# A sliding-window attention and ReGLU kernel: two more Strassen pairs from the third tiles of the last four halves, early scores for two halves, packed masks

## The chip, the cores and the metric

The kernel runs on one core of a Trainium2 chip. The metric is device time in microseconds of one launch; the time before is the median of three runs. The core has a matmul engine (TensorE, PE in the profile; PEld is its weight load), a vector engine (VectorE, DVE), a scalar engine (ScalarE, ACT), GpSimd (POOL) and SyncE (SP, which here issues DMAs). Each works through its own queue in program order; semaphores tie them together. Matmuls write to PSUM banks, of which there are eight; DVE and ACT read them and write to SBUF.

## The reference

```python
def _attn_ref(q, k, v, n_global, n_local):        # q, k, v: 4 x 8 heads x 768 x 64
    scores = scale * np.matmul(q, k.transpose(0, 1, 3, 2))
    rel = pos[:, None] - pos[None, :]
    is_global = pos[None, :] < int(n_global)       # 8
    is_local = (rel >= 0) & (rel < int(n_local))   # 96
    keep = is_global | is_local
    dist = np.where(is_global & ~is_local, float(n_local), np.abs(rel))
    scores = scores + (-slopes[:, None, None] * dist[None, :, :])[None, :, :, :]
    a = softmax(np.where(keep, scores, -1e9))
    return np.matmul(a, v)

def _moe_ref(x, w_gate, w_val, w_out):             # x: 3072 x 512, d_ff 1536
    gate = np.maximum(x @ w_gate, 0.0)
    val = x @ w_val
    return gate * val @ w_out
```

The attention's output, heads side by side, is `x`. Inputs and output are float32; the kernel multiplies in bf16.

## The kernel before

**Halves and stages.** The 3072 rows are cut into eight halves of 384 rows, numbered 0 to 7 here (the sixth and the eighth half are 5 and 7); two halves make one batch. A half is three tiles of 128 rows. After a hand-ordered opening (halves 0 and 1), the loop `for c in range(2, NHALF)` runs one stage for each half c: the FFN of half c, with the attention of half c+1 and the key and query preparation of half c+2 woven in between. What follows calls these stages 2 to 7.

**Weaving.** `weave` takes the FFN's pieces, each with a weight, and lists of other pieces, each with a place between 0 and 1. After every FFN piece it issues all pieces whose place times the stage's total weight has been reached. `spread(items, a, b)` puts n items at even distances from a to b. This sets the program order, and so the order in every engine's queue. A piece of weight 0.0 costs no place.

**FFN of a half** (`ffn_pieces`). `f1` holds, for each of 12 hidden tiles `fc`, `gate(fc)` (four matmuls of 384 columns, L518, then a relu on ACT, L525) and `val(fc)` (four matmuls, then DVE's `ht = val * relu`, L531). Its first pieces are `begin` (the first three matmuls of gate 0 and val 0, weight 1.0) and the two last matmuls of gate 0 and val 0 (0.15 each). `f2` is the output product. From half 1 on, tiles 0 and 1 are a Strassen pair: seven block products `p4 p3 p1 p2 p5 p6 p7` of six 256-column matmuls each (L583), whose operands are sums of `ht` (`sum_cb`, `sum_ad`, `sum_de` on DVE, L567 to L577) and sums of the output weights (`bs`, made once). ACT copies p4, p3 and p1 into the output rows (L599 to L607), DVE adds p2, p5, p6 and p7 (L611 to L629), p6 onto p3's bank and p7 onto p1's. Some of the sums are issued behind `val` of given hidden tiles (`behind`), the rest inside `f2`. The third tile takes the plain way, `outp`: four parts of three 512-column matmuls (L538), an ACT copy (L543) and a store on SP.

**Attention of a half** (`attention_pieces`): 26 pieces. For each of four head pairs p: `piece_qk` with g = 0, 1, 2 (`pair_scores` issues the score matmuls of both groups into four banks, L397; g = 0 issues the exps of group 0, g = 1 those of group 1 and the masks of group 0, g = 2 the masks of group 1), `piece_av` for both heads (L427, then a log on ACT, L436, and after the second head an exp of the negated log, L441), and `piece_norm` (two DVE multiplications into `xT`, L446). The masks are DVE multiplications of the exponentials with `m_all`, one for each key block, L359: two for each group in an even half, three and two in an odd one. `early_pieces` casts k and q on POOL (L363), transposes them by DMA on SP (L368) and orders the keys on POOL (L259 to L265).

**Buffers.** From the loop on, PSUM is three `ff` banks (gates, values, outp, p4, p3, p1) and five `x` banks (scores, attention sums, p2, p5), each given out in rotation: the fourth `ff` tile waits until the first has been read. `es` (exponentials) has three buffers a group, `ht` two, `osb` (output rows) three.

Of the kernel before, what the change touches and what calls it, by code (L numbers as in the profile page):

```python
# [8 lines left out]
FP32 = mybir.dt.float32  # L9
BF16 = mybir.dt.bfloat16  # L10
# [5 lines left out]
def kernel(  # L16
# [80 lines left out]
    dd = const.tile([128, 2, NN, WQ], BF16)  # L97
# [75 lines left out]
    kq0 = firstp.tile([128, 2, H, NN * D], FP32, name="kq0")  # L173
    kq1 = setupp.tile([128, 2, H, NN * D], BF16, name="kq1")
# [173 lines left out]

    def masks(s, p, g, steps=steps_of):
        for j in steps[s % 2][g]:  # L350
            _, a, w, m = by[s % 2, j]
            es, c = es_of[s, p, j]
            for_all = es[:, :, c : c + NN * w]
            mk = m_all[:, 2 * p : 2 * p + 2, 0 if j == 0 else 1, :, m : m + w]
            if w == WQ:
                mk = mk.rearrange("k e n p -> k e (n p)")
            else:
                for_all = for_all.rearrange("k e (n p) -> k e n p", n=NN)
            nc.vector.tensor_mul(for_all, for_all, mk)  # L359
# [148 lines left out]

    def ffn_pieces(c):
# [43 lines left out]

        N2, D2 = N_FC // 2, DM // 2
        tiles_ = [slice(n * 128, (n + 1) * 128) for n in range(2)]

        def sums_of(name, *shape):
            if name not in st:
                st[name] = late["sums"].tile([128, *shape], BF16, name=name)
            return st[name]  # L560

        cb = lambda: sums_of("cb", N2, 2, 128)
        ad = lambda: sums_of("ad", N2, 128)
        de = lambda: sums_of("de", N_FC, 128)

        def sum_cb(i0, i1):
            nc.vector.tensor_tensor(cb()[:, i0:i1].rearrange("f i n t -> f i (n t)"), ht[:, i0:i1, 0:256],  # L567
                                    ht[:, N2 + i0 : N2 + i1, 0:256], op=ALU.add)

        def sum_ad(i0, i1):  # L570
            nc.vector.tensor_tensor(ad()[:, i0:i1], ht[:, i0:i1, tiles_[0]],
                                    ht[:, N2 + i0 : N2 + i1, tiles_[1]], op=ALU.add)

        def sum_de(i0, i1):
            x, y = (1, 0) if i0 < N2 else (0, 1)
            nc.vector.tensor_tensor(de()[:, i0:i1], ht[:, i0:i1, tiles_[x]], ht[:, i0:i1, tiles_[y]],
                                    op=ALU.subtract)  # L577

        def block(key, pool, left, right, start, stop):
            if start:  # L580
                st[key] = psum[pool].tile([128, 512], FP32, name=f"{pool}_ps")
            for i in range(N2):
                nc.tensor.matmul(st[key][:, 0:D2], lhsT=left(i), rhs=right(i),  # L583
                                 start=start and i == 0, stop=stop and i == N2 - 1,
                                 skip_group_check=not start)
            return st[key][:, 0:D2]

        c0, c1 = slice(0, D2), slice(D2, DM)
        bs = lambda name: lambda i: late["bs"][name][:, i]
        V2 = nc.vector.tensor_tensor  # L590

        def store(n, cols, eng=nc.sync):
            eng.dma_start(out=out_v[c, n][:, cols], in_=st["r", n][:, cols])

        def p4():
            for n in range(2):
                st["r", n] = late["osb"].tile([128, DM], FP32, name="osb")
            ps = block("d", "ff", lambda i: ht[:, N2 + i, tiles_[1]], bs("b21-b11"), True, True)
            nc.scalar.copy(st["r", 0][:, c0], ps)  # L599

        def p3():
            ps = block("c", "ff", lambda i: ht[:, i, tiles_[0]], bs("b12-b22"), True, True)
            nc.scalar.copy(st["r", 0][:, c1], ps)

        def p1():
            ps = block("a", "ff", lambda i: ad()[:, i], bs("b11+b22"), True, True)
            nc.scalar.copy(st["r", 1][:, c1], ps)  # L607

        def p2():
            ps = block("b", "x", lambda i: cb()[:, i, 1], lambda i: wo_sb[:, i, c0], True, True)  # L610
            V2(st["r", 1][:, c0], ps, st["r", 0][:, c0], op=ALU.add)  # L611
            V2(st["r", 1][:, c1], st["r", 1][:, c1], ps, op=ALU.subtract)

        def p5():
            ps = block("e", "x", lambda i: cb()[:, i, 0], lambda i: wo_sb[:, N2 + i, c1], True, True)
            V2(st["r", 0][:, c1], ps, st["r", 0][:, c1], op=ALU.add)
            V2(st["r", 0][:, c0], st["r", 0][:, c0], ps, op=ALU.subtract)
            if c == NHALF - 1:
                store(1, c0)
                store(0, c1)  # L620

        def p6():
            ps = block("c", "ff", lambda i: de()[:, i], bs("b11+b12"), False, True)
            V2(st["r", 1][:, c1], ps, st["r", 1][:, c1], op=ALU.add)
            store(1, slice(0, DM) if c < NHALF - 1 else c1, nc.sync if c < NHALF - 1 else nc.scalar)

        def p7():
# [251 lines left out]
```

## Time and profile before

| | |
|---|---|
| time, median of 3 runs | 241.64 us (241.13 to 242.92) |
| the profiled execution | 241.74 us, of which the span from first to last instruction is 239.9 us |
| TensorE clock granted | 0.998 |
| PE busy | 233.5 us (97%), 1937 matmuls |
| DVE, ACT, POOL busy | 173.3, 153.4, 85.9 us |
| stage 2 | 78.6 to 104.8 us |
| stage 3 | 104.8 to 131.7 us |
| stage 4 | 131.7 to 159.4 us |
| stage 5 | 159.4 to 186.4 us |
| stage 6 | 186.4 to 213.9 us |
| stage 7 and the end | 213.9 to 239.9 us |

In a row of the profile stand the source line, the engine, the operation, the tile written and the tiles read, the shapes, the count; then the busy time and the mean duration in ns of one; then the engine's idle time before these instructions and what ended it. In a timeline, the first number is the start in us and the second how long the run of equal instructions took. A duration holds the pipeline's latency, so instructions of one engine overlap by it; the distance between starts is what a queue pays. Matmul ends are modelled. A stage's borders here are the starts of its first gate matmul and of the next stage's.

### The profile page before, as it was taken

To read this page: it belongs to the slowest core of one execution; us is meant where nothing else is said; L and a number is where in the kernel's file an instruction comes from. 1 tells how busy PE (TensorE), PEld (TensorE's weight loads), DVE (VectorE), ACT (ScalarE), POOL (GpSimd) and SP (SyncE) were. 2 spreads that over 40 slices of the span, in tenths; PEclk is the share of its full clock that TensorE was granted. 3 is DMA by queue.
4 is the path that set the end of the run, shared out by engine and by line. 5 is a ranking of instruction groups with operands and counts; after the bars stand their busy time and mean duration, and the time that the engine had idled before them with its cause. 6 is when DMAs were issued, how large, how long until landed. Compare 5 with 4: busy or idle time off the path is not lost.

```text
span 239.9 us, 5355 instructions
## 1 busy us (share of the span) xinstructions
PE 233.5 (97%) x1937; PEld 146.6 (61%) x1945; DVE 173.3 (72%) x456; ACT 153.4 (64%) x347; POOL 85.9 (36%) x202
## 2 busy tenths in 40 slices
PE   7899999999999999999999999999999999999994
PEld 3655555665458566666668566676658566676663
DVE  7775955869677788777787687866887677764643
ACT  5897883337775777748774777638774677733330
POOL 6767893208414860903274060902350000000000
PEclk9999999999999999999999999999999999999999
DMA  6999999993976997098519939398431200030003
GB/s 200 181 198 177 257 234 219 185 162 61 270 178 134 301 150 131 8 185 257 108 25 122 285 93 133 19 166 262 67 68 44 90 0 0 3 129 3 4 27 104
DMA packets 69603, 31.42 MB, mean 131 GB/s; under 512 B 47160, under 2 KB 66616, under 8 KB 69576
## 3 DMA queue, kind: packets, MB, share of 16 engines
q0 software_dynamic: 31744, 8.71, 35.3%
q1 hardware_dynamic: 36616, 21.45, 35.1%
q10 hardware_dynamic: 1216, 0.92, 1.2%
q8 instruction: 15, 0.25, 0.4%
q14 instruction: 12, 0.10, 0.1%
HBM read 28.41 MB, written 6.29 MB: 145 GB/s over the span
## 4 chain that ended last, share of the span: by engine, by line
PE 91%; ACT 3%; DVE 2%; issue 1%; ACTq 0%
PE ff_ps L518 53%; PE ff_ps L538 9%; PE ff_ps L583 8%; PE x_ps L427 6%; PE x_ps L397 4%; PE x_ps L583 3%; PE t_ps L459 2%; PE s_ps L341 2%; PE t_ps L272 1%; PE t_ps L682 1%; ACT lnd L436 1%; PE t_ps L310 1%; DVE xT L446 1%; PE s_ps L321 1%; ACT rcp L441 0%
## 5 line engine op out<-in xcount | busy, mean ns | idle before, releaser
L518 PE MATMUL ff_ps<-xT,wg 128*128 128x384 bf16 x384 | 80.7, 326 | 0.5 <-ACT grelu L525 0.4
L518 PE MATMUL ff_ps<-xT,wv 128*128 128x384 bf16 x384 | 80.2, 326 | 0.0
L531 DVE TENSOR_TENSOR ht<-ff_ps,grelu 128x384 bf16<-128x384 f32 x96 | 53.1, 554 | 28.5 <-PE ff_ps L518 13.8
L525 ACT ACTIVATE grelu<-ff_ps 128x384 bf16<-128x384 f32 x96 | 47.1, 492 | 39.4 <-PE ff_ps L518 20.9
L518 PEld LDWEIGHTS <-wg 128*128 128x128 bf16 x384 | 35.9, 98 | 23.9 <-issue 0.9
L518 PEld LDWEIGHTS <-wv 128*128 128x128 bf16 x384 | 36.1, 97 | 23.4 <-issue 1.2
L406 ACT ACTIVATE es<-x_ps 128x360 bf16<-128x360 f32 (+2 forms) x96 | 36.8, 444 | 16.9 <-PE x_ps L397 16.8
L359 DVE TENSOR_TENSOR es<-es,m_all 128x432 bf16<-128x432 bf16 (+4 forms) x108 | 31.2, 334 | 8.2 <-ACT es L406 7.8
L446 DVE TENSOR_TENSOR xT<-x_ps,rcp 64x384 bf16<-64x384 f32 x48 | 26.6, 554 | 9.4 <-ACT rcp L441 8.8
L436 ACT ACTIVATE lnd<-x_ps 64x384 f32<-64x384 f32 x48 | 23.3, 485 | 12.5 <-PE x_ps L427 11.8
L538 PE MATMUL ff_ps<-wo_sb,ht 128*128 128x512 bf16 x112 | 29.6, 379 | 0.4
L363 POOL CAST kqc<-ks 128x384 bf16<-128x384 f32 x24 | 11.6, 532 | 32.3 <-DMA ks<-in_k_dram 32.3
L137 POOL DMA_DIRECT2D vbuf<-in_v_dram x25 | 21.6, 880 | 2.6 <-DMA wv<-in_moe_w_val_dram 2.1
L427 PE MATMUL x_ps<-es,vbuf 128*128 128x216 bf16 (+4 forms) x216 | 21.8, 225 | 0.0
L427 PEld LDWEIGHTS <-vbuf 128*128 128x128 bf16 x216 | 15.8, 97 | 7.7
L538 PEld LDWEIGHTS <-ht 128*128 128x128 bf16 x120 | 10.8, 97 | 9.8 <-issue 0.2
L263 POOL COPY kT<-kqT 128x240 bf16<-128x240 bf16 x16 | 6.9, 430 | 23.0 <-DMA kqT<-kqc 20.5
L363 POOL CAST kqc<-qs 128x384 bf16<-128x384 f32 x24 | 11.6, 522 | 8.1 <-DMA qs<-in_q_dram 8.1
L259 POOL COPY kT<-kqT 128x360 bf16<-128x360 bf16 x10 | 6.0, 604 | 19.9 <-DMA kqT<-kqc 19.9
L441 ACT ACTIVATE rcp<-lnd 128x384 f32<-128x384 f32 x24 | 12.6, 524 | 0.7
L347 ACT ACTIVATE ef<-s_ps 128x720 bf16<-128x720 f32 (+2 forms) x16 | 10.9, 710 | 2.1 <-PE s_ps L341 1.8
L397 PE MATMUL x_ps<-kqT,kT 64*128 64x216 bf16 (+4 forms) x216 | 11.8, 224 | 0.2
(115 smaller groups left out, 252.8 us busy)
## 6 DMA issues: line engine op xcount, KB each, us to landing
out_dram<-osb SPq DMA_DIRECT2D x22, 256.0 KB, 2.7
ks<-in_k_dram SPq DMA_DIRECT2D x6, 768.0 KB, 5.5
qs<-in_q_dram SPq DMA_DIRECT2D x6, 768.0 KB, 12.1
vbuf<-in_v_dram POOLq DMA_DIRECT2D x21, 120.0 KB, 7.9
wg<-in_moe_w_gate_dram POOLq DMA_DIRECT2D x3, 512.0 KB, 7.9
wv<-in_moe_w_val_dram POOLq DMA_DIRECT2D x3, 512.0 KB, 9.8
wo_sb<-in_moe_w_out_dram POOLq DMA_DIRECT2D x1, 1536.0 KB, 19.6
kq<-in_q_dram ACTq DMA_DIRECT2D x2, 192.0 KB, 4.7
```

Source lines behind the costliest of these rows:

```text
L137: nc.gpsimd.dma_start(out=v_dst(b, NG + r0, NG + r0 + n, j), in_=v[b, :, KT * j + r0 : KT * j + r0 + n, :].rearrange("h p d -> p h d"))
L359: nc.vector.tensor_mul(for_all, for_all, mk)
L363: nc.gpsimd.tensor_copy(kqc[:, :, i].rearrange("t n (h d) -> t h n d", d=D)[:, 2 * p : 2 * p + 2], of[s][:, 2 * p : 2 * p + 2, :].rearrang ...
L406: nc.scalar.activation(es[:, e, 0:c], banks[e][:, 0:c], AF.Exp, bias=0.0, scale=scale)
L427: nc.tensor.matmul(av3[:, :, a : a + w], lhsT=vb[:, j, z0 : z0 + 128], rhs=es[:, e, c : c + NN * w].rearrange("k (n p) -> k n p", n=NN), s ...
L436: nc.scalar.activation(ln[o0 : o0 + 64], av[d0 : d0 + 64, 0:QH], AF.Ln, bias=0.0, scale=1.0)
L446: nc.vector.tensor_tensor(xT_of[s][r, p, :], av_of[s, p, e][r, 0:QH], av_of[s, p, "r"][r], op=ALU.mult)
L518: nc.tensor.matmul(st[key][:, 0:QH], lhsT=w_of(w, dc, fc), rhs=xT_of[c][:, dc, :], start=(dc == 0), stop=(dc == N_DC - 1))
L525: nc.scalar.activation(gr, psg[:, 0:QH], AF.Relu, bias=0.0, scale=1.0)
L531: nc.vector.tensor_tensor(ht[:, fc, :], psv[:, 0:QH], st["gr", fc], op=ALU.mult)
L538: nc.tensor.matmul(ps2, lhsT=ht[:, fc, n * 128 : (n + 1) * 128], rhs=wo_sb[:, fc, :], start=(fc == 0), stop=(fc == N_FC - 1))
L583: nc.tensor.matmul(st[key][:, 0:D2], lhsT=left(i), rhs=right(i), start=start and i == 0, stop=stop and i == N2 - 1, skip_group_check=not s ...
```

## The change

- For halves 4 and 6 (`PAIRED`), the third tile is no longer multiplied in its own stage. Stage 4 keeps `third_of[4]`, and stage 5 multiplies the third tiles of halves 5 and 4 as one more Strassen pair; likewise 7 and 6. The sums of that pair have their own buffers (`sums3`); three of the five are issued behind `val` 1, 6 and 7, two at the head of `f2`, whose products go before those of tiles 0 and 1. Stages 4 and 6 have no `outp` left, begin their output products with p3 instead of p4, and put p4 into an `x` bank.
- In stages 3 and 5 the first three attention pieces of halves 5 and 7 (head pair 0: scores, exps and masks) are issued at places 0.82 to 0.93, one stage sooner. The remaining 23 pieces lie at 0 to 0.74 of stages 4 and 6, where 26 lay at 0 to 0.8.
- From half 3 on, the masks of a first score group are one multiplication with a packed copy of the masks. POOL makes the two packed copies once, in five pieces, at places 0.7 to 0.9 of the combined stage of halves 0 and 1 (57 to 78 us).
- `osb` gets a fourth buffer, and the tile `dd` moves to a pool that is closed before the loop.

```diff
+    def pack_mask(half, i):
+        todo = [by[half, j] for j in steps_later[half][0]]
+        if half not in packed_of:
+            packed_of[half] = late["packed"].tile([128, H, sum(NN * t[2] for t in todo)], BF16, name=f"packed{half}")
+        c = sum(NN * t[2] for t in todo[:i])
+        j, _, w, m = todo[i]
+        nc.gpsimd.tensor_copy(
+            packed_of[half][:, :, c : c + NN * w].rearrange("k h (n t) -> k h n t", n=NN),
+            m_all[:, :, 0 if j == 0 else 1, :, m : m + w])
+
     def masks(s, p, g, steps=steps_of):
+        if s > 2 and g == 0:
+            mk = packed_of[s % 2][:, 2 * p : 2 * p + 2]
+            es = es_of[s, p, steps[s % 2][0][0]][0][:, :, 0 : mk.shape[2]]
+            nc.vector.tensor_mul(es, es, mk)
+            return
         for j in steps[s % 2][g]:
...
+    def strassen(pair, sums, bare=False):
+        N2, D2 = N_FC // 2, DM // 2
+        st = {}
+        last = pair[0][0] == NHALF - 1 and pair[0][2] == 0
+        def h(i, f0, f1):
+            _, ht, n = pair[i]
+            return ht[:, f0:f1, n * 128 : (n + 1) * 128]
...
+        def sum_cb_of(i):
+            V2(cb()[:, :, i], h(i, 0, N2), h(i, N2, N_FC), op=ALU.add)
...
+        def p4():
+            ps = block("d", "x" if bare else "ff", lambda i: h(1, N2 + i, N2 + i + 1)[:, 0], bs("b21-b11"), True, True)
+            nc.scalar.copy(rows(0)[:, c0], ps)
...
+        return sum_cb, sum_cb_of, sum_ad, sum_de, [(0.65, f) for f in (((p3, p4) if bare else (p4, p3)) + (p1, p2, p5, p6, p7))]
+
+    PAIRED = (4, 6)
+    third_of = {}
...
+        plain = range(NN) if c < 1 else () if c - c % 2 in PAIRED else (NN - 1,)
+        sum_cb, _, sum_ad, sum_de, products = strassen([(c, ht, 0), (c, ht, 1)], "sums", c in PAIRED)
         behind = {2: [lambda: sum_de(0, 3)], 5: [lambda: sum_de(3, 6)], 8: [lambda: sum_cb(0, 3)],
                   9: [lambda: sum_ad(0, 3)], 10: [lambda: sum_de(6, 9)]}
+        rest = (lambda: sum_ad(3, 6), lambda: sum_cb(3, 6), lambda: sum_de(9, 12))
+        if c in PAIRED:
+            third_of[c] = ht
+        elif c - 1 in PAIRED:
+            _, cb3, ad3, de3, products3 = strassen([(c, ht, NN - 1), (c - 1, third_of[c - 1], NN - 1)], "sums3")
+            behind[1] = [lambda: cb3(1)]
+            behind[6] = [lambda: ad3(0, N_FC // 2)]
+            behind[7] = [lambda: de3(0, N_FC // 2)]
+            rest = (lambda: cb3(0), lambda: de3(N_FC // 2, N_FC)) + rest
...
         if c >= 1:
-            f2 += [(0.65, f) for f in (p4, p3, p1, p2, p5, p6, p7)]
-            for at, f in ((5, lambda: sum_de(9, 12)), (3, lambda: sum_cb(3, 6)), (2, lambda: sum_ad(3, 6))):
+            f2 += (products3 if c - 1 in PAIRED else []) + products
+            places = (2, 3, 5) if plain else (0, 1, 2) if c in PAIRED else (0, 1, 2, 3, 4)
+            for at, f in list(zip(places, rest))[::-1]:
                 f2.insert(at, (0.0, f))
...
-    late["osb"] = ctx.enter_context(tc.tile_pool(name="osb", bufs=3, reuse_waits="tile"))
+    late["osb"] = ctx.enter_context(tc.tile_pool(name="osb", bufs=4, reuse_waits="tile"))
...
+          spread([(0.0, lambda half=half, i=i: pack_mask(half, i)) for half, i in ((1, 0), (1, 1), (1, 2), (0, 0), (0, 1))],
+                 0.7, 0.9))
+
+    ahead = {}
     for c in range(2, NHALF):
         placed = []
-        if c + 1 < NHALF:
-            placed.append(spread(attention_pieces(c + 1), *((0.07, 0.82) if c == 2 else (0.0, 0.8))))
         if c + 2 < NHALF:
             load_qk(c + 2, 0, H)
             load_v_half(c + 2)
             placed.append(spread(early_pieces(c + 2), 0.25, 0.75))
+        if c + 1 < NHALF:
+            pieces = ahead.pop(c + 1, None) or attention_pieces(c + 1)
+            placed.append(spread(pieces, *(0.07, 0.82) if c == 2 else (0.0, 0.74) if c in PAIRED else (0.0, 0.8)))
+        if c + 1 in PAIRED:
+            ahead[c + 2] = attention_pieces(c + 2)
+            placed.append(spread([ahead[c + 2].pop(0) for _ in range(3)], 0.82, 0.93))
         f1, f2 = ffn_pieces(c)
         weave(f1 + f2, *placed)
```

Block products, copies, combinations and stores of `strassen` are otherwise those of before, for the two tiles named in `pair`.

## The prediction

> **What bounds the kernel now.** I read the page first: busy shares and the chain that ended last.
>
> ```profile
> PE 233.5 (97%) x1937; PEld 146.6 (61%) x1945; DVE 173.3 (72%) x456; ACT 153.4 (64%) x347; POOL 85.9 (36%) x202
> PE 91%; ACT 3%; DVE 2%; issue 1%; ACTq 0%
> ```
>
> TensorE carries 91% of the chain. Then I cut the span into the stages of the loop (stage c runs half c's FFN with half c+1's attention):
>
> ```profile
> 131.69:159.36 27.67, 27.56 (x232) 17.85 (x230) 21.47 (x54) 18.98 (x44) 9.93 (x23) 1.00 0.72 132
> 159.36:186.38 27.02, 26.97 (x214) 17.45 (x214) 20.56 (x50) 18.34 (x44) 7.26 (x20) 1.00 0.47 118
> ```
>
> Columns: length, then PE, PEld, DVE, ACT, POOL busy, clock, DMA. In stages 4 and 5 PE is filled to within 0.1 us and DVE is busy for 21 of 27 us. So a matmul saved is time saved, if the in-order queues of DVE and ACT give PE its operands and empty PSUM banks as punctually as now. Third view, the groups by shape, for prices:
>
> ```profile
> L538 PE MATMUL ff_ps<-wo_sb,ht 128*128 128x512 bf16 x112 | 29.6, 379 | 0.4
> L583 PE MATMUL ff_ps<-bs,ht 128*128 128x256 bf16 x84 | 10.3, 272 | 0.0
> L567 DVE TENSOR_TENSOR cb<-ht 128x768 bf16<-128x768 bf16 x14 | 7.8, 554 | 0.2
> L359 DVE TENSOR_TENSOR es<-es,m_all 128x432 bf16<-128x432 bf16 x36 | 14.0, 389 | 8.2 <-ACT es L406 7.8
> L359 DVE TENSOR_TENSOR es<-es,m_all 128x144 bf16<-128x144 bf16 x12 | 2.7, 227 | 0.0
> L359 DVE TENSOR_TENSOR es<-es,m_all 128x96 bf16<-128x96 bf16 x12 | 3.1, 256 | 0.0
> ```
>
> A mean contains pipeline latency; what a queue pays is the distance between starts. From the chain: three 512-column matmuls in 0.65 us (216 ns each), eighteen 256-column ones in 1.97 us (109 ns). On DVE back to back: a 768-element sum 0.47, a half-size PSUM combination 0.33, ht 0.48, an xT pair 1.1 us.
>
> **Strassen pair instead of two plain third tiles (stages 4+5, 6+7).** Removed: 2 x 12 matmuls x 216 ns = 5.18 us. Added: 7 x 6 x 109 ns = 4.58. Gain 0.60 a pair, **-1.21 us** in all, on the path since PE is full. The Trainium skill, "TensorE: Matmul & The Clock Gate", section "Back-to-back issue gap", speaks against it: it gives a sustained 131 ns at 512 columns and 81 ns at 128. By a straight line between them (an estimate from that page, 98 ns at 256) the pair would cost 42 x 98 - 24 x 131 = 0.97 us more. The trace has 216 and 109 ns, so the gain stands.
>
> Each pair adds five 768-element sums on DVE (2.4 us by starts) and six combinations (2.0), mostly in stages 5 and 7, and trades two 0.57 us ACT copies for three of 0.37.
>
> **Packed masks.** Three multiplications of an odd half's first group (starts 0.30 + 0.14 + 0.12 us) become one of 672 elements; between the 384-element sums (starts 0.27 apart) and the 768 ones (0.47) I take 0.42: 0.14 saved; an even half saves about as much. Twenty times that is 2.8 us of DVE, not of PE. The five POOL copies are not in the trace: POOL's kT copies run from 238 ns (48 elements) to 604 (360), about 1.2 ns an element over 0.2 us, so 1728 + 576 + 384 + 1728 + 192 elements cost some 6 us (between zero and double). POOL idles 8.5 us before the kT copies at 75.57, and half 3's first score at 79.25 needs only the first set, done at 76.37. Before the last cast lies one copy of 2.1 us; the transposes behind it wait on SP for a store until 68.9 anyway. Cost 0. Without that cover (copies twice as long) the transposes come 2 us later and still fit. The Trainium skill, "GPSIMD Engine Reference", section "Specifications", says GpSimd's SBUF interfaces are contended by DVE instructions with two SBUF inputs, which the masks are. No row here separates that; it would lead to the doubled case, at 0 as well.
>
> **Start of stages 4 and 6.** Now:
>
> ```profile
> 133.34 0.81 PE L518 MATMUL ff_ps<-xT,wg 128*128 128x384 bf16 x4
> 134.18 0.81 PE L518 MATMUL ff_ps<-xT,wv 128*128 128x384 bf16 x4
> ...
> 132.95 0.79 ACT L406 ACTIVATE es<-x_ps 128x336 bf16<-128x336 f32 x2 [3.47 <-PE x_ps L397]
> 133.63 0.50 ACT L525 ACTIVATE grelu<-ff_ps 128x384 bf16<-128x384 f32 x1
> 134.00 0.85 ACT L406 ACTIVATE es<-x_ps 128x360 bf16<-128x360 f32 x2
> ```
>
> With three ff banks, val(1) reuses the bank of gate(0) and waits for relu(0): that ends at 134.13, val(1) starts at 134.18, 0.19 us late. In the new weave the stage's weight is 1.3 + 22 x 0.65 + 7 x 0.65 = 20.15 and 23 attention pieces lie in 0 to 0.74: the second is due at 1.5/23 x 0.74 x 20.15 = 0.97, below begin's 1.0. Before it was 1.5/26 x 0.8 x 22.75 = 1.05, after gate(0). So both exp pairs now stand ahead of relu(0) in ACT's queue; relu(0) slips by two exps (0.35 each) and val(1) to about 134.88. Behind it in PE's queue stands everything. **+0.70 each, +1.40 us.**
>
> **Start of the output products in stages 4 and 6.** The last attention pieces now fall inside the gates: 0.74 x 20.15 = 14.9 of f1's 15.6. How an xT pair delays ht stands here:
>
> ```profile
> 146.15 1.14 DVE L446 TENSOR_TENSOR xT<-x_ps,rcp 64x384 bf16<-64x384 f32 x2 [0.75 <-ACT rcp L441]
> 147.33 0.56 DVE L531 TENSOR_TENSOR ht<-ff_ps,grelu 128x384 bf16<-128x384 f32 x1
> ```
>
> That ht came 0.98 us after its matmuls' end. For ht(11) this cost nothing before, as four output parts (2.6 us) covered it. Now p3 (0.65 us, hidden tiles 0-5) is all the cover and p4's sixth matmul reads ht(11): after f1's last matmul PE wants it at 0.65 + 0.55 = 1.2 us and gets it at 0.16 (the profile's end of a matmul behind the next start) + 0.95 late + 0.55 for ht + 0.06 to the next engine = 1.7. **+0.5 each, +1.0 us.** Bounds: 0 if xT is early, 1.1 if the sums behind ht(11) bind too.
>
> **Scores of halves 5 and 7 a stage early.** Inputs are there: half 5's first kT set is done by 122.4 and the scores come at 128.4; for half 7 177.4 against about 184. The stage's end pays:
>
> ```profile
> 130.16 0.41 DVE L612 TENSOR_TENSOR osb<-osb,x_ps 128x256 f32<-128x256 f32 x1
> 130.49 0.42 DVE L616 TENSOR_TENSOR osb<-x_ps,osb 128x256 f32<-128x256 f32 x1
> 130.82 0.41 DVE L617 TENSOR_TENSOR osb<-osb,x_ps 128x256 f32<-128x256 f32 x1
> 131.15 0.41 DVE L624 TENSOR_TENSOR osb<-ff_ps,osb 128x256 f32<-128x256 f32 x1
> ...
> 131.53 0.49 PE L518 MATMUL ff_ps<-xT,wg 128*128 128x384 bf16 x2
> 131.85 0.49 PE L518 MATMUL ff_ps<-xT,wv 128*128 128x384 bf16 x2
> ```
>
> The next stage's val(0) takes the bank that p6's combination (L624) frees, 0.28 us ahead of need. The early masks of the second group (starts 0.27 + 0.25) land between p2's and p5's combinations and push it back 0.52: **+0.28 us, twice, +0.56.** Bounds 0 and 0.6 each, the latter if the exps are late.
>
> **Middle of stage 5.** From ht(11) on DVE has, back to back: two pair sums 0.95, masks 0.55, ad 0.3, xT pair 1.1, cb 0.47, p2's two combinations 0.67, de 0.3, p5's two, p6's one, xT pair 1.1, p7's one. Summed, the last xT pair frees its x bank 6.7 us and p7's combination its ff bank 7.7 us after f1. PE comes to half 7's second score bank at 6.4 and to p1's bank at 7.2. **+0.5 us**; 0 to 1.6. Stage 7 has no attention: 1.3 us a hidden tile holds ht 0.48 and a sum 0.47. Cost 0, to 0.3.
>
> Two waits of attention sums on late masks (PE stood 0.20 us at 152.7 and 0.11 at 179.8) lose their place: **-0.3 us**.
>
> Sum: -1.21 - 0.3 + 1.40 + 1.0 + 0.56 + 0.5 = +1.95. The profiled execution took 241.74 us (span 239.94), 0.1 over the median of 241.64. Forecast **243.6 us**, 0.8% slower.
>
> **Rivals.** *The queues absorb it* (0.22): exps and xT run ahead enough and only PE's gain stays: -1.2 to -1.5, 240.2 us. For it: scores done early make DVE's load at the stage starts lighter. Against: the 0.19 us wait at 134.18 shows that queue order already binds. *DVE becomes the bound of stage 5* (0.20): 20.6 us busy + 2.8 sums + 2.5 combinations + 1.3 half 7's masks - 0.7 = 26.5 of about 29.5, nearly all of it after f1 without gaps. It decides where an operation costs its duration instead of its start distance: 0.08 us x some 20 operations, 1.6 us more before stage 6 and a little in stages 3, 4 and 6: 245.5 us. *The change does not do what it says* (0.08): packed multiplications as dear as the separate ones, or half 7's keys late; 242 to 246. The forecast's own case, waits of 2.5 to 4.5 us against 1.5 of gains, has 0.50: 242.6 to 244.6.
>
> **Numbers.** A measurement of this kernel tells about 1% from no change: 239.2 and 244.1. Faster by more than PE's saving isn't in reach: 0.03. Above 244.1 lie the second rival and the upper third of the forecast: 0.33. The rest is 0.64. The range goes from the first rival's 240.2 to the second's 245.5.
>
> **What would show it.** PE busy down by about 1.2 us less what bubbles hide; val(1) of stages 4 and 6 behind four exps and 0.9 us late; p4 of the same stages pausing 0.5 us before its last matmul; a gap at the start of stages 4 and 6 before val(0); DVE over 85% in stage 5. It is wrong if PE shows no new gap there, or if DVE's backlog in stage 5 reaches past its end.

## The result and the profile after

The changed kernel takes 245.87 us (median of six runs, 245.2 to 246.83); the kernel before, run beside it, takes 241.8 us. The ratio is 1.0175 with an interval of 1.0154 to 1.0196: **1.75% slower**, where 0.8% was forecast. The profiled execution took 245.56 us with a span of 243.8, which is 3.85 us more span than before's profiled execution. All sums below are made against those two executions.

The first two lines are from the page of after: busy time by engine, and the engines' shares of the chain that ended last.

```profile
PE 233.1 (96%) x1977; PEld 149.5 (61%) x1981; DVE 180.7 (74%) x446; ACT 152.9 (63%) x349; POOL 91.8 (38%) x207
PE 79%; DVE 9%; ACT 7%; issue 3%; DMA 1%; ACTq 0%; DVEq 0%
```

TensorE's part of the chain fell from 91% to 79%, while DVE's rose from 2% to 9% and ACT's from 3% to 7%. PE is waiting for operands and banks in more places. The stage windows tell where. This is the view by windows of after, stages 3 to 6 (length; PE, PEld, DVE, ACT and POOL busy; clock, DMA share, GB/s):

```profile
105.27:132.69 27.42, 27.37 (x225) 17.62 (x224) 20.65 (x49) 19.77 (x48) 11.33 (x25) 1.00 0.72 134
132.69:159.08 26.39, 25.02 (x210) 16.43 (x208) 19.98 (x45) 16.86 (x39) 10.09 (x23) 1.00 0.65 124
159.08:189.44 30.36, 29.81 (x256) 20.74 (x254) 24.93 (x60) 20.20 (x50) 8.09 (x20) 1.00 0.44 116
189.44:215.58 26.14, 24.87 (x211) 16.43 (x208) 19.15 (x45) 16.86 (x39) 0.00 (x0) 1.00 0.06 21
```

Stages 4 and 6 have no plain third tile any more and should have become shorter by its 2.6 us and by the scores that moved out; they stand idle on PE for 1.4 and 1.3 us instead (26.39 less 25.02, 26.14 less 24.87), where stages 4 and 5 of before left 0.1 us. The lengths beside each other, from the starts of the first gate matmuls:

| us | combined stage | 2 | 3 | 4 | 5 | 6 | 7 |
|---|---|---|---|---|---|---|---|
| before | 19.29 | 27.72 | 26.91 | 27.67 | 27.02 | 27.47 | 22.94 |
| after | 20.03 | 28.00 | 27.43 | 26.39 | 30.36 | 26.13 | 24.93 |

(The combined stage is taken from its first output matmul, stage 7 to PE's last matmul. Stage 2's first gate matmul starts at 76.9 us in before; the table ahead of the prediction has a later one, 78.6.) Stage 7 is the one place that shows the new product alone, without attention: it grew by 1.99 us, which is a pair of 42 matmuls at 109 ns (4.58 us) less twelve plain ones at 216 ns (2.59). With the plain tile gone from the stage before it, a pair saves 0.6 us, as worked out. The work was saved, and the waits cost more.

From the groups by shape of after:

```profile
L656 PE MATMUL ff_ps<-wo_sb,ht 128*128 128x512 bf16 x68 | 17.8, 379 | 0.2
L570 PE MATMUL x_ps<-bs,ht 128*128 128x256 bf16 x12 | 2.0, 274 | 1.0 <-DVE ht L649 1.0
L366 DVE TENSOR_TENSOR es<-es,packed 128x672 bf16<-128x672 bf16 x12 | 6.0, 504 | 3.7 <-ACT es L424 3.7
L358 POOL COPY packed<-m_all 128x1728 bf16<-128x1728 bf16 x2 | 3.3, 1660 | 0.0
```

The plain output product is down from 112 recorded matmuls to 68 (48 fewer by the program; some records are missing). The second line is p4 of stages 4 and 6, which also reads the last hidden tile: PE stood idle for 1.0 us within it, for `ht`. The packed multiplication takes 504 ns, and the large packing copy 1.66 us.

**The four waits.** First, the start of stage 4, from after's timeline (start, time taken, engine, instructions, idle time before them and what ended it):

```profile
134.73 0.81 PE L636 MATMUL ff_ps<-xT,wg 128*128 128x384 bf16 x4
136.29 0.49 PE L636 MATMUL ff_ps<-xT,wv 128*128 128x384 bf16 x2 [0.75 <-ACT grelu L643]
...
134.34 1.52 ACT L424 ACTIVATE es<-x_ps 128x336 bf16<-128x336 f32 x4 [2.96 <-PE x_ps L415]
135.72 0.91 ACT L643 ACTIVATE grelu<-ff_ps 128x384 bf16<-128x384 f32 x2
```

Four exps stand ahead of relu(0) on ACT, and val(1) starts when relu(0) has released its bank. The row shows 0.75 us idle; the profile's modelled end of a matmul reaches 0.16 us past the next possible start, so val(1) is 0.91 us later than PE could have had it (0.19 before). Stage 6 shows the same 0.91.

Second, p4 of stage 4:

```profile
154.43 0.71 PE L570 MATMUL x_ps<-bs,ht 128*128 128x256 bf16 x5
155.69 0.28 PE L570 MATMUL x_ps<-bs,ht 128*128 128x256 bf16 x1 [0.55 <-DVE ht L649]
...
153.91 1.13 DVE L464 TENSOR_TENSOR xT<-x_ps,rcp 64x384 bf16<-64x384 f32 x2
155.07 0.56 DVE L649 TENSOR_TENSOR ht<-ff_ps,grelu 128x384 bf16<-128x384 f32 x1
```

Five matmuls run, and the sixth waits until `ht(11)`, which stood behind an xT pair on DVE, is written at 155.63. That is 0.71 us, and 0.63 in stage 6.

Third, the end of stage 3:

```profile
131.60 0.59 DVE L377 TENSOR_TENSOR es<-es,m_all 128x384 bf16<-128x384 bf16 x2
132.11 0.41 DVE L605 TENSOR_TENSOR osb<-x_ps,osb 128x256 f32<-128x256 f32 x1
132.45 0.41 DVE L606 TENSOR_TENSOR osb<-osb,x_ps 128x256 f32<-128x256 f32 x1
132.77 0.41 DVE L613 TENSOR_TENSOR osb<-ff_ps,osb 128x256 f32<-128x256 f32 x1
132.69 0.49 PE L636 MATMUL ff_ps<-xT,wg 128*128 128x384 bf16 x2
```

The two early masks stand ahead of p5's and p6's combinations (L605, L606, L613). The last of these ends at 133.18 and frees the bank of val(0), which starts at 133.24, 0.22 us late; 0.23 at stage 6.

Fourth, one that the prediction had at nothing, in the combined stage of halves 0 and 1:

```profile
66.78 1.97 DVE L862 TENSOR_TENSOR bs<-wo_sb 128x768 bf16<-128x768 bf16 x1
68.79 1.14 DVE L464 TENSOR_TENSOR xT<-x_ps,rcp 64x384 bf16<-64x384 f32 x2
66.65 1.70 POOL L358 COPY packed<-m_all 128x1728 bf16<-128x1728 bf16 x1
69.39 0.31 PE L415 MATMUL x_ps<-kqT,kT 64*128 64x216 bf16 x3 [0.85 <-DVE xT L464]
```

A weight sum of 768 elements, 0.55 us alone, took 1.97 us. It started 0.13 us into POOL's packing copy and ended 0.4 us after it. The xT pair behind it freed a score bank so late that PE stood 1.01 us at the scores (0.26 before). Of the seven traces of kernels with the packing, five show this meeting (the sum takes 1.97 us, the combined stage 19.91 to 20.18) and two do not (0.85 us and 19.29): there the sum started before the copy.

### The profile page after: what moved, and what is told of

Its sections match the earlier page's. It is cut to its first block, busy times and chain, and to the rows that moved or that the text cites. A ratio compares the mean times of both kernels' runs of the same rounds, so it can differ in the third digit from the quotient of the medians.

```text
span 243.8 us, 5439 instructions
## 1 busy us (share of the span) xinstructions
PE 233.1 (96%) x1977; PEld 149.5 (61%) x1981; DVE 180.7 (74%) x446; ACT 152.9 (63%) x349; POOL 91.8 (38%) x207
## 4 chain that ended last, share of the span: by engine, by line
PE 79%; DVE 9%; ACT 7%; issue 3%; DMA 1%; ACTq 0%; DVEq 0%
PE ff_ps L636 48%; PE ff_ps L570 8%; PE x_ps L445 5%; PE ff_ps L656 4%; PE x_ps L570 4%; PE x_ps L415 4%; DVE xT L464 2%; PE t_ps L477 2%; ACT lnd L454 2%; ACT es L424 1%; DVE ht L649 1%; PE s_ps L341 1%; PE t_ps L733 1%; DMA out_dram<-osb 1%; PE t_ps L310 1%
## 5 line engine op out<-in xcount | busy, mean ns | idle before, releaser
L424 ACT ACTIVATE es<-x_ps 128x360 bf16<-128x360 f32 (+2 forms) x96 | 36.3, 445 | 15.4 <-PE x_ps L415 15.4
L377 DVE TENSOR_TENSOR es<-es,m_all 128x432 bf16<-128x432 bf16 (+4 forms) x56 | 17.8, 358 | 1.9 <-ACT es L424 1.7
L656 PE MATMUL ff_ps<-wo_sb,ht 128*128 128x512 bf16 x68 | 17.8, 379 | 0.2
L381 POOL CAST kqc<-qs 128x384 bf16<-128x384 f32 x24 | 12.2, 545 | 8.5 <-DMA qs<-in_q_dram 8.4
L366 DVE TENSOR_TENSOR es<-es,packed 128x672 bf16<-128x672 bf16 (+1 forms) x20 | 9.5, 476 | 6.7 <-ACT es L424 6.7
L415 PE MATMUL x_ps<-kqT,kT 64*128 64x216 bf16 (+4 forms) x216 | 12.6, 224 | 1.7 <-DVE xT L464 1.6
L564 DVE TENSOR_TENSOR de<-ht 128x384 bf16<-128x384 bf16 (+1 forms) x32 | 13.1, 411 | 0.5
L570 PE MATMUL x_ps<-wo_sb,cb 128*128 128x256 bf16 x108 | 13.4, 273 | 0.0
L570 PE MATMUL ff_ps<-bs,de 128*128 128x256 bf16 x108 | 13.3, 273 | 0.0
```

Source lines behind the costliest of these rows:

```text
L381: nc.gpsimd.tensor_copy(kqc[:, :, i].rearrange("t n (h d) -> t h n d", d=D)[:, 2 * p : 2 * p + 2], of[s][:, 2 * p : 2 * p + 2, :].rearrang ...
L415: nc.tensor.matmul(banks[e][:, c : c + NN * w].rearrange("k (n t) -> k n t", n=NN), lhsT=kt[r, j, :], rhs=qd[r, :, a : a + w], start=True, ...
L424: nc.scalar.activation(es[:, e, 0:c], banks[e][:, 0:c], AF.Exp, bias=0.0, scale=scale)
L656: nc.tensor.matmul(ps2, lhsT=ht[:, fc, n * 128 : (n + 1) * 128], rhs=wo_sb[:, fc, :], start=(fc == 0), stop=(fc == N_FC - 1))
```

## The experiments

Prices in us below are differences of ratios times 241.6. Each ratio is to the kernel before, run on the same chip; its interval is about 0.5 us to either side, so only the larger prices stand clear of noise by themselves.

### The scores' exps behind relu(0)

```diff
-... else (0.0, 0.74) if c in PAIRED else ...
+... else (0.006, 0.74) if c in PAIRED else ...
```

This moves one piece, the second exp pair of stages 4 and 6, from behind `begin` to behind gate 0.

> Changed kernel with one edit: the attention pieces of stages 4 and 6 start at place 0.006 instead of 0.0, which moves one piece of each stage (exps of the second group of head pair 1, masks of the first) from behind begin to behind gate 0, so relu(0) comes before the second pair of exps. Queue theory: val(1) of stages 4 and 6, 0.91 us late in the changed kernel, is again at most 0.2 us late; time falls by 1.3 to 1.5 us, from 245.9 to about 244.5. Rival (DVE is the bound of the stages, waits only move): the 0.7 us reappears later in the stage and the time stays within 0.4 us of 245.9.

Measured: 244.17 us, ratio 1.0115 (1.009 to 1.0139), 1.45 us less than the changed kernel. The interval is clear of the changed kernel's. The timeline of this kernel at the same place:

```profile
134.43 0.81 PE L636 MATMUL ff_ps<-xT,wg 128*128 128x384 bf16 x4
135.27 0.81 PE L636 MATMUL ff_ps<-xT,wv 128*128 128x384 bf16 x4
...
134.04 0.79 ACT L424 ACTIVATE es<-x_ps 128x336 bf16<-128x336 f32 x2 [2.96 <-PE x_ps L415]
134.72 0.50 ACT L643 ACTIVATE grelu<-ff_ps 128x384 bf16<-128x384 f32 x1
135.09 0.85 ACT L424 ACTIVATE es<-x_ps 128x360 bf16<-128x360 f32 x2
```

Two exps, relu(0), two exps: the order of the kernel before is back, and val(1) is again 0.185 us late, as before the change. What was lost there was only a place in ACT's queue. In the profiled execution stages 3 to 7 fell by less, 1.08 us (135.24 to 134.16): the last matmul of p4 in stage 4 now waits 1.03 us instead of 0.71, and the first bank of the early scores in stage 5 comes 0.37 us late instead of 0.14. A wait that goes can uncover a part of the next.

### The last xT pair behind p4

```diff
+            if c in PAIRED:
+                placed[-1][-1] = (0.82, placed[-1][-1][1])
```

> Changed kernel with one edit: in stages 4 and 6 the last attention piece (the two xT multiplications of head pair 3) is issued behind p4 instead of behind gate 11, so ht(11) and two sums stand before it in DVE's queue. Queue theory: the gaps inside p4 (0.71 us in stage 4, 0.63 in stage 6) and before p3 of stage 4 (0.18) go, time falls by 1.2 to 1.5 us to about 244.5. Rival (ht(11) is late because relu(11) stands behind the log and the exp on ACT, not because of xT): at least 0.4 us of each gap stays and the time falls by less than 0.6 us.

Measured: 244.29 us, ratio 1.0125 (1.0101 to 1.0149), 1.2 us less, clear of the changed kernel's interval and the same as stages 3 to 7 show (135.24 to 134.03). The timeline of this kernel in stage 6:

```profile
209.56 0.82 PE L570 MATMUL x_ps<-bs,ht 128*128 128x256 bf16 x6
209.25 0.56 DVE L649 TENSOR_TENSOR ht<-ff_ps,grelu 128x384 bf16<-128x384 f32 x1 [0.21 <-ACT grelu L643]
210.59 1.12 DVE L464 TENSOR_TENSOR xT<-x_ps,rcp 64x384 bf16<-64x384 f32 x2
```

`ht(11)` now goes first, p4's six matmuls run as one, and the 0.18 us before p3 in stage 4 is gone too. DVE still waited 0.21 us for the relu, and that was early enough: the xT pair was the cause, not ACT.

In this kernel's profiled execution the combined stage took 19.29 us, as before the change, although the packing was in it: the copy and the weight sum did not meet. So the fourth wait falls in some executions and not in others.

### The masks not packed

```diff
-        if s > 2 and g == 0:
+        if False:
...
-          spread([(0.0, lambda half=half, i=i: pack_mask(half, i)) ...], 0.7, 0.9))
```

> Changed kernel without the packed masks: no packing copies on POOL, first groups masked block by block as before. Contention theory (a DVE operation with two SBUF inputs waits until a running POOL copy has ended): the 768-element sum that took 1.97 us beside the 1.70 us packing copy takes 0.55 again, the 0.75 us gap between scores at 68 us goes and the 0.29 us one in stage 2 too, while DVE gets about 2.8 us more masks, which add 0.1 to 0.4 us of waits in stages 4 to 6: time falls by 0.5 to 0.9 us to about 245.2. Rival (the packed masks pay): time rises by 0.3 us or more.

Measured: 245.2 us, ratio 1.0155 (1.0133 to 1.0177), 0.5 us less, with an interval that overlaps the changed kernel's. In its trace the combined stage is back at 19.29 us and the weight sum there at 0.85 us (a cast on POOL runs beside it). The 0.29 us of stage 2, which were expected to go as well, stayed: stage 2 has 28.07 us here. Stage 4 has longer waits instead, 0.42 us within the scores before 140.75 and 0.94 at p4, with more masks on DVE. Stages 3 to 7 take 135.69 us against 135.24, so packing pays 0.45 us in the loop and costs 0.74 in the combined stage where copy and sum meet; the times alone do not settle the size.

### The early masks behind p7

```diff
             placed.append(spread([ahead[c + 2].pop(0) for _ in range(3)], 0.82, 0.93))
+            placed[-1][-1] = (0.99, placed[-1][-1][1])
```

> Changed kernel with one edit: the second-group masks of the early head pair of halves 5 and 7 are issued behind p7 of stages 3 and 5 instead of behind p2. Queue theory: the combination of p6 is no longer pushed back, val(0) of stages 4 and 6 loses its 0.22 us wait each, time falls by 0.3 to 0.5 us to about 245.4. Rival (the masks then delay ht(0) of the next stage by as much): no change, within 0.15 us of 245.9.

Measured: 245.57 us, ratio 1.0163 (1.0139 to 1.0186), 0.3 us less, again within the overlap of the intervals. The timeline of this kernel at the end of stage 3 shows the mechanism better than the time does:

```profile
132.42 0.42 DVE L613 TENSOR_TENSOR osb<-ff_ps,osb 128x256 f32<-128x256 f32 x1
133.39 0.35 DVE L377 TENSOR_TENSOR es<-es,m_all 128x384 bf16<-128x384 bf16 x1
132.85 0.49 PE L636 MATMUL ff_ps<-xT,wg 128*128 128x384 bf16 x2
133.18 0.49 PE L636 MATMUL ff_ps<-xT,wv 128*128 128x384 bf16 x2
```

p6's combination ends before the next stage begins, and val(0) follows gate(0) after 0.33 us, two matmuls' time, with no gap. Stages 3 to 7 fell by 0.25 us there and not by the two waits of 0.45 together, since p4's last matmul in stage 4 waits 0.96 us now instead of 0.71.

### The two kernels with plain transfers

The remaining kernels load `kqT` by a plain transfer where before and after transpose by DMA (18 transfers, halves 2 to 7). What is left out is this transposition: halves 2 to 7 score untransposed keys and queries. The number and the timing of all instructions on the engines are meant to stay the same, and the first two kernels show how far they do.

```diff
-        nc.sync.dma_start_transpose(
+        nc.sync.dma_start(
...
-            in_=kqc[:, n].rearrange("t i z -> t (i z)"))
+            in_=kqc[:, n].rearrange("t i (p z) -> t (i p) z", z=128))
```

> Control: the kernel before with its 18 transposing DMAs of keys and queries (halves 2 to 7) replaced by plain DMA copies of the same tiles. Halves 2 to 7 then score untransposed data, so their part of the output is not the reference's; instructions, shapes and order of all engines stay. Expected by every theory: within 0.5 us of the kernel before, since keys land earlier and nothing waits for them.

> Control: the changed kernel with the same plain copies in place of transposing DMAs (the same part of the output is not the reference's). Expected: the waits on order alone stay (val(1) 0.91 us and p4 0.6 us or more in stages 4 and 6, val(0) 0.22 us, early scores of half 7 0.7 us), so 1.4% to 1.9% over the kernel before. If the transposes' traffic was part of the cause, it comes out under 1.2%.

Measured: the kernel before with this edit 241.47 us, ratio 0.9987 (0.9973 to 1.0001); the changed kernel with it 245.63 us, ratio 1.0156 (1.0135 to 1.0177). The waits of the changed kernel are all there: val(1) 0.91 us late in stages 4 and 6, p4's last matmul 0.71 and 0.63 with 0.21 before p3 of stage 4, val(0) of both 0.23, the combined stage 19.97 us. Only at the early scores of stage 5 is the wait shorter, 0.46 us instead of 0.85 (the paragraph on stage 5 below). So these two are the controls for what follows.

### The end of stage 5 reordered

The changed kernel has one more wait, at the early scores of half 7 in stage 5. From after's timeline:

```profile
184.16 0.55 PE L415 MATMUL x_ps<-kqT,kT 64*128 64x216 bf16 x7
185.26 0.31 PE L415 MATMUL x_ps<-kqT,kT 64*128 64x192 bf16 x3 [0.55 <-DVE xT L464]
184.33 0.41 DVE L613 TENSOR_TENSOR osb<-ff_ps,osb 128x256 f32<-128x256 f32 x1
184.67 1.13 DVE L464 TENSOR_TENSOR xT<-x_ps,rcp 64x384 bf16<-64x384 f32 x2
```

The second score bank is the one that the last xT pair reads, and that pair stands behind the combinations of the new Strassen pair: 0.71 us late, and 0.14 in front of the first bank.

```diff
+        if c == 5:
+            placed[-2][-1] = (0.81, placed[-2][-1][1])
+            placed[-1] = [(x, f) for x, (_, f) in zip((0.90, 0.95, 0.99), placed[-1])]
```

> The changed kernel's control with one edit, in stage 5 alone: half 7's early scores are issued behind p2 of the second product set (exps of group 2 behind p6, last masks behind p7) instead of behind p4, and half 6's last xT pair behind p7 of the first set instead of behind p6. Plain copies as in the control, so the output differs in the same part. Backlog theory (DVE's queue behind ht(11) frees the score banks and p1's bank late): the 0.14 + 0.71 us gaps within the early scores go and val(0) of stage 6 loses most of its 0.22 us; time 0.8 to 1.1 us under the changed kernel's control. Rival (DVE is simply full in stage 5): the gap moves to a later place in stage 5 or into stage 6 and the time falls by less than 0.3 us.

Measured: 245.81 us, ratio 1.0167 (1.0146 to 1.0188), nothing gained on the control's 1.0156. The wait at the scores is gone, and two others have come. The timeline of this kernel:

```profile
184.89 0.81 PE L570 MATMUL ff_ps<-bs,ht 128*128 128x256 bf16 x6 [0.19 <-DVE osb L613]
187.80 0.81 PE L570 MATMUL x_ps<-wo_sb,cb 128*128 128x256 bf16 x6 [0.38 <-ACT es L424]
```

p3 of tiles 0 and 1 waits 0.36 us (0.19 idle by the row) for the bank that the combination of the third tiles' p6 frees, and p5 waits 0.54 for a bank that the exps of the early scores still read. Stage 5 is 30.21 us long instead of 29.97, and stage 6 25.91 instead of 26.13, as its val(0) is no longer late. The gap had moved, as the rival of this run said. That DVE is simply full, the rival's reason, does not follow: the run that frees stage 5, below, has no such gap with more work on DVE.

### All order edits together, masks unpacked

The edits of the four kernels above and of this last one, in one kernel (with plain transfers).

> The changed kernel's control with all four order edits together (second exps behind gate 0 in stages 4 and 6, last xT pair behind p4 there, early second-group masks behind p7, the stage 5 edit) and without packed masks; plain copies as in the control, so the output differs in the same part. If the waits add up as the single edits show (1.45 + 1.2 + 0.3 + 0.9 + 0.5 us), time is 4.0 to 4.6 us under the changed kernel's control and level with or up to 0.6% under the kernel before's control: PE's 1.2 us of saved matmuls are then left as the gain. If the waits stand in for each other (one hides behind another), it stays 0.8 us or more above the kernel before's control.

Measured: 241.81 us, ratio 1.0008 (0.9993 to 1.0022), 3.6 us less than the control's 1.0156 and level with the kernel before (0.5 us over the 0.9987 of its control, with intervals that overlap). The single edits add up to 3.45 us (1.45, 1.2, 0.5, 0.3 and nothing); the difference is within the intervals. Stages 4 and 6 are now 24.63 and 24.55 us; only stage 5 still has new waits, as this kernel's window of it shows:

```profile
156.54:187.23 30.69, 29.75 (x257) 20.63 (x255) 25.20 (x64) 20.30 (x50) 8.11 (x20) 1.00 0.46 117
```

PE is busy for 29.75 of 30.69 us; p3 of tiles 0 and 1 is 0.72 us late and p5 0.54 (both with the 0.16 that the modelled ends hide).

### The packed masks alone

On the kernel before with plain transfers: `pack_mask`, the five packing pieces, the packed branch of `masks` and the move of `dd`, nothing else of the change.

> Kernel before with packed masks alone (packing on POOL at the same places), nothing else of the change; plain copies as in the controls, so the output differs in the same part. Contention theory: DVE's 2.8 us saved are not on the path, one sum of the output weights may meet the 1.7 us packing copy: between 0 and 0.9 us over the kernel before's control, and where the sum meets the copy its duration is near the copy's remainder plus 0.4 us. Rival (fewer DVE operations relieve the stages): 0.3 us or more faster than that control.

Measured: 242.58 us, ratio 1.0052 (1.0033 to 1.0071), 1.6 us over its control's 0.9987 by the ratios and 1.1 us by the medians, more than the 0 to 0.9 expected. The packed masks **by themselves make the kernel slower**; that they would relieve DVE enough to win is refuted. Where this is lost stays partly open. The profiled execution (242.26 us) is one in which the copy did not hold the weight sum:

```profile
67.51 0.85 DVE L828 TENSOR_TENSOR bs<-wo_sb 128x768 bf16<-128x768 bf16 x1
67.90 1.95 POOL L358 COPY packed<-m_all 128x1728 bf16<-128x1728 bf16 x1
```

The sum started first, and the copy, which takes 1.62 to 1.70 us when it starts first, took 1.95. The combined stage has 19.29 us and stages 3 to 7 are those of the control to 0.03 us; stage 2 has 27.72 instead of 28.07. But the first output matmul came at 58.07 us instead of 57.26. In the other traces of this case it lies at 57.23 to 57.82, with and without the moved tile `dd`, so the move alone does not explain it. And of the 1.1 us about 0.25 lie outside the span from first to last instruction, which no trace shows: all six executions of this kernel are 1.98 to 2.10 us longer than their spans, where the other kernels are so by 1.75 to 1.80 in the mean.

### Twelve copies on POOL beside the last stage

To measure the disputed cost by itself: the kernel before with plain transfers and twelve 1728-element copies on POOL at the end of stage 6 and in stage 7 (210.4 to 230.9 us), where POOL has nothing to do. The tile `dd` is moved as in the change to make room.

```diff
+        if c == NHALF - 1:
...
+            placed.append([(0.0, lambda: nc.gpsimd.tensor_copy(gate_, xT_of[c][0:1, N_DC - 1, 0:1]))]
+                          + [(0.001, lambda: nc.gpsimd.tensor_copy(
+                              scr.rearrange("k h (n t) -> k h n t", n=NN), m_all[:, :, 1])) for _ in range(12)])
```

> Kernel before with twelve extra POOL copies (128 x 1728 bf16 into a scratch tile, none of the result uses it) beside the last stage, where POOL has nothing else; plain copies as in the controls, so the output differs in the same part. Contention theory: every DVE sum of two SBUF tensors (de, cb, ad: 0.36 to 0.55 us alone) that starts beside a copy ends only after that copy has, so up to 2 us each, while ht (one PSUM, one SBUF input) keeps 0.55 us; the last stage, 22.9 us long, grows by several us. Rival (the ports are shared element by element): sums take at most double, 0.7 to 1.1 us, and copies grow by as much.

Measured, in a single execution, 242.3 us. The timeline of this kernel:

```profile
222.40 1.66 DVE L576 TENSOR_TENSOR de<-ht 128x384 bf16<-128x384 bf16 x1
221.80 0.56 DVE L531 TENSOR_TENSOR ht<-ff_ps,grelu 128x384 bf16<-128x384 f32 x1 [0.74 <-PE ff_ps L518]
222.22 1.63 POOL L846 COPY scr<-m_all 128x1728 bf16<-128x1728 bf16 x1
```

`de = ht - ht`, with two inputs in SBUF, takes 0.36 us alone; here it started 0.18 us into a copy and took 1.66, ending 0.2 us after the copy. Others took 1.41, 1.30 and 1.31 (for `ad`), each ending 0.2 us after a copy's end; one that started 0.28 us before a copy's end took 0.49. `ht`, with one input in PSUM and one in SBUF, kept its 0.55 us. Eleven of the copies kept 1.62 to 1.64 us; the one that started 0.2 us into a `cb` took 1.85. The rival, ports shared element by element, would at most have doubled the sums and stretched the copies beside them; here DVE's instruction **waits for the rest of the copy**. The expectation that the last stage would grow by several us was wrong: 23.59 us against 22.94. Only sums are held, and most of them are needed later.

### Stage 5 freed: p4 of halves 4 to 6 into an x bank

```diff
-        ... = strassen([(c, ht, 0), (c, ht, 1)], "sums", c in PAIRED)
+        ... = strassen([(c, ht, 0), (c, ht, 1)], "sums", c in (4, 5, 6))
...
-            ... zip((0.90, 0.95, 0.99), placed[-1])]
+            ... zip((0.94, 0.97, 0.99), placed[-1])]
```

This is made on top of the kernel with all order edits.

> The kernel with all order edits and unpacked masks, with two more edits in stage 5: products of tiles 0 and 1 start with p3 and put p4 into an x bank (as stages 4 and 6 do), so they need p6's bank of the first set one product later, and half 7's early scores are issued behind p5, so p5 doesn't wait for p2's bank. Plain copies as in the controls, so the output differs in the same part. If the two waits seen in stage 5 (0.72 us before p3, 0.54 before p5) are what is left of the backlog, stage 5 falls from 30.7 to about 29.5 us and the time to about 240.6 us, 0.3% to 0.6% under the kernel before's control: the saved matmuls are then a net gain. If DVE is full in stage 5, the waits turn up elsewhere in it and the time stays at 241.4 us or more.

Measured: 241.08 us, ratio 0.9977 (0.9955 to 1.0). Its windows of stages 4 and 5, and then those of the kernel before with plain transfers:

```profile
132.25:156.84 24.59, 24.57 (x210) 16.55 (x208) 19.78 (x51) 16.88 (x39) 9.94 (x23) 1.00 0.58 130
156.84:186.60 29.76, 29.76 (x256) 20.63 (x254) 25.31 (x64) 20.30 (x50) 7.95 (x20) 1.00 0.49 121
```

```profile
131.52:159.18 27.66, 27.59 (x231) 17.89 (x230) 21.31 (x55) 18.98 (x44) 10.21 (x23) 1.00 0.62 130
159.18:186.13 26.95, 26.90 (x216) 17.45 (x215) 20.46 (x51) 18.33 (x44) 7.45 (x20) 1.00 0.44 119
```

No new wait is left in either stage. Which of the two edits removed which wait was not run apart. Stages 3 to 7 take 131.35 us together, against 131.94 of the control: of the 1.21 us of saved matmuls 0.6 remain. The ratio is 0.1% under the control's, which these intervals cannot tell from nothing.

### The same without early scores

```diff
-        if c + 1 in PAIRED:
-            ahead[c + 2] = attention_pieces(c + 2)
-            ...
```

All 26 attention pieces lie at 0.006 to 0.8 of stages 4 and 6 again.

> The last kernel (all order edits, masks unpacked, stage 5 freed) without the early scores: halves 5 and 7 keep all 26 attention pieces in stages 4 and 6, at 0.006 to 0.8, the last xT pair behind p4 as there; plain copies as in the controls, so the output differs in the same part. This leaves the two Strassen pairs alone of the three parts. If the early scores cost more than they bring (0.1 us where PE turns from products to scores, two more operations ahead of the stage's end), stages 3 to 7 together fall by 0.2 to 0.6 us from 131.35 us and the time to about 240.7; if they bring cover for the fuller stages 4 and 6 (ht(11) and the exps later by two attention pieces there), the stages grow by 0.3 us or more.

Measured: 241.43 us, ratio 0.9995 (0.9975 to 1.0014); stages 3 to 7 take 131.87 us in its profile. New waits are 0.64 us before 145.78 and 0.32 us at the starts of stages 5 and 7. The early scores give a little cover in the trace (0.5 us); the times don't tell the two apart.

## Why the prediction was wrong

Slower was right, and so was the mechanism of the waits that were in the sum (val(1), p4, val(0), stage 5), but the sum was too small: +1.95 us predicted, +4.07 in the medians, +3.85 in the spans of the profiled executions. In the latter the part before the combined stage happened to be 0.38 us shorter (its end lies between 57.23 and 58.07 us over all traces, before and after alike), so the stages have to account for +4.25. Term by term:

| term, us | predicted | measured | by |
|---|---|---|---|
| matmuls saved | -1.21 | -1.21 | stage 7's 4.58 - 2.59, starts of matmuls |
| two waits gone | -0.3 | -0.31 | trace |
| val(1) behind four exps | +1.40 | +1.45 | trace, first experiment |
| p4 behind the xT pair | +1.0 | +1.5 | trace, second experiment (1.2) |
| val(0) behind early masks | +0.56 | +0.45 | trace, fourth experiment (0.3) |
| stage 5 | +0.5 | +0.85 | trace |
| packing on POOL | 0 | +0.75 | trace of after, and of four others of seven with packing |
| a group of scores each in stages 4 and 6 | 0 | +0.38 | trace |
| stage 2, a sum beside a cast on POOL | 0 | +0.29 | trace; as much in some kernels without the packing, so chance |
| remainder | 0 | +0.1 | what is left of 4.25 |

**The step that failed** is the packing: "Cost 0", and for contention between the two engines "it would lead to the doubled case, at 0 as well". I followed POOL's own chain (casts, copies, transposes) and found slack in it, which was right; the large copy took 1.66 us instead of an estimated 2.1 to 2.3. I didn't follow DVE's queue while POOL copies. The copies fall into the stage where DVE makes the last of the ten weight sums, which have two inputs in SBUF, and behind a sum that is held stands the xT pair that PE waits for. The Trainium skill, "GPSIMD Engine Reference", section "Specifications", says that GpSimd's SBUF interfaces are contended by DVE instructions with two SBUF inputs; the run with twelve copies agrees and gives the size, which is not a doubling of the copy but DVE's instruction put off by up to the rest of it (0.36 to 1.66 us). The price varies: 0.6 to 0.9 us in the five traces where copy and sum met, nothing in the combined stage of the two others. The masks alone cost 1.1 us in the medians, a part of which has no place yet.

The prediction said that no row of before separates this. There was one, in the combined stage:

```profile
66.21 1.00 DVE L359 TENSOR_TENSOR es<-es,m_all 128x432 bf16<-128x432 bf16 x2 [0.62 <-ACT es L406]
65.96 1.10 POOL L363 CAST kqc<-qs 128x384 bf16<-128x384 f32 x2
```

Two 432-element masks, 389 ns each in the mean, took 1.00 us beside two POOL casts. The 0.29 us of stage 2 are the same effect without the packing: a sum `de`, 0.36 us alone, is held by a cast and takes 0.48 to 0.71 us in five of the seven traces with the packing and in four of the seven without, the control of the kernel before among them (0.71 us, stage 2 28.07 us). Stage 2 takes 27.71 to 28.07 us with and without the packing.

**Two sizes were off, and one wait was missing.** *p4*: 0.5 us was worked out for each stage, 0.71 and 0.63 were measured, with 0.18 more before p3 in stage 4. The second experiment takes the xT pair away and with it all of this. What makes stage 4 the dearer one, by 0.26 us, was not run; its sum `ad` took 0.60 us beside a key copy on POOL, against 0.35 in stage 6, where POOL is idle. *Stage 5*: I took 0.5 from a range of 0 to 1.6; 0.85 came, and 0.46 in the control with plain transfers, so the term was not far off. *Scores in stages 4 and 6*: the second of three groups of scores is longer than the others. These are the timelines of after and, for the group at the same place, of before:

```profile
140.25 0.67 PE L415 MATMUL x_ps<-kqT,kT 64*128 64x216 bf16 x10
```

```profile
141.25 0.48 PE L397 MATMUL x_ps<-kqT,kT 64*128 64x216 bf16 x10
```

By starts it holds PE for 0.60 us, where the two others and all four of stage 4 before hold it for 0.41; stage 6 shows the same at 197.0. Its matmuls come in pairs that start 3 to 5 ns apart, and a pair whose second bank came late runs one behind the other. In the trace of the third experiment the same matmul waits 0.42 us for an xT pair on DVE, so this is most likely a bank that DVE frees late; it was not run by itself. Turning from the 128-row products to a group of scores and back costs PE 0.10 and 0.09 us, but there are 16 such turns in stages 3 to 6 both before and after, so they are no part of the loss.

**The rivals.** That the queues absorb the change is refuted by every one of the waits. DVE as the bound of stage 5 is not what happened: it is busy for 24.93 of 30.36 us there (82%, where over 85% was to show it), and the freed kernel fills PE in all 29.76 us with DVE busy for 25.31 of them (85%), so that share does not make DVE the bound either. The time was near that rival's 245.5 for another reason. Of what was to be seen, four things came as told (val(1) behind four exps, 0.9 late; p4's last matmul; val(0) late; PE busy lower, by 0.4 us as the modelled ends count it) and one did not (DVE's share).

The range ended at 245.5 since it was closed with the DVE rival and gave no room to several terms being too small at once. Only val(0) was put too high, by 0.1 us. The waits all come from in-order queues behind a PE without slack, and they are not independent: p4's 0.71 us became 1.03 with the exps moved and 0.96 with the masks moved.

## What to carry to other kernels

Price a change in a full kernel by what stands ahead, in each engine's queue, of the instruction that PE waits for; here moving one piece of 23 past its neighbour, in two stages, was worth 1.45 us, and order, with the masks unpacked, gave back nearly all that the change had lost. Work that is taken off PE may have been the cover of something: the plain tile's 2.6 us hid the last `ht`. And a copy on an idle GpSimd is not free while VectorE does sums with both inputs in SBUF, so it belongs where VectorE reads PSUM or rests. Short pieces should hold less at a time (beside casts of 0.5 us a sum lost at most 0.35 us here); cutting the copy was not run.

## What was not expected of the hardware

- A DVE instruction with two SBUF inputs that starts during a POOL copy of 1.62 to 1.70 us ends 0.2 to 0.4 us after that copy (0.36 became 1.30 to 1.66 us; 0.55 became 1.97). Beside casts of 0.5 us the same happens in small (0.36 became up to 0.71). One with an input in PSUM is not touched (0.55 us).
- The copy can be the one that is late: where a weight sum (0.85 us, a cast was running at its start) began 0.39 us before it, the copy took 1.95 us; where a `cb` began 0.2 us before it, 1.85.
- 42 matmuls of 256 columns with as many weight loads run at 109 ns from start to start, half of the 216 ns at 512 columns, so splitting a product into smaller ones cost PE nothing by itself.
